# A new written-out order, with other engines and added dummy matmuls, for a fused linear-attention and MLP kernel

## The chip, the cores and the metric

The kernel runs on one core of one Trainium2 chip. A core has a matrix engine (PE, with its weight loads shown as PEld), VectorE (DVE in the profile), ScalarE (ACT), GpSimd (POOL) and SyncE (SP), which here only issues transfers. Each engine takes its instructions in the order in which the program gives them to it. The metric is the device time of one execution in microseconds (us), lower is better.

## What is computed

Inputs are r, k and v of shape (4, 8, 768, 48), that is batch, heads, sequence and head width, per-head decays w and gains u, and the weights of a small MLP on d = 384 channels. First comes a linear attention with a decaying state, then a layer norm, an MLP with ReLU and a residual sum:

```python
for t in range(S):
    kt, vt, rt = (k[:, :, t].copy(), v[:, :, t].copy(), r[:, :, t].copy())
    cur = np.einsum('bhd,bhe->bhde', u[None] * kt, vt)
    y[:, :, t] = np.einsum('bhd,bhde->bhe', rt, state + cur)
    state = w[None, :, :, None] * state + np.einsum('bhd,bhe->bhde', kt, vt)
...
mu = np.mean(x, axis=-1, keepdims=True)
var = np.mean((x - mu) ** 2, axis=-1, keepdims=True)
xn = (x - mu) / np.sqrt(var + 1e-06) * g_ln
ch = np.maximum(xn @ w_ch1, 0.0) @ w_ch2
return (x + ch).astype(np.float32)
```

## The kernel before

The sequence is cut into chunks of 128 steps. There are 6 chunks for each of 4 batches, 24 in all, numbered so that chunk i belongs to batch i mod 4 and follows chunk i - 4. Inside a chunk the recurrence is turned into matmuls: r is scaled by powers of w (Fr) and k by the inverse powers (Fk), a masked product A gives the part from within the chunk, and a state Z, carried from chunk i - 4, gives the rest. The MLP works on groups of one or two chunks (17 groups; groups 6 to 12 hold two), so that its matmuls have 128 or 256 columns.

Everything is written as small named steps, and the string `PLAN` lists them. An entry such as `SK,3,g` names the step, its index and the engine that does it: v is VectorE, s ScalarE, g GpSimd, and - means that the step has only one possible engine. A loop at the end calls one function for each entry:

```python
for step in PLAN.split():
    name, i, e = step.split(",")
    steps[name](int(i), e)
```

So the position in the string is the order on every queue at once. A load that stands late in the string is issued late by SP, and a PE step whose input is late holds up all PE steps after it. No scheduler reorders anything. The pools of buffers (`SLOTS`) say how far loads may run ahead: 11 buffers each for k, r and v.

The steps, in the order in which a chunk meets them:

- WF and WB load the row of w and spread it over 128 partitions with a matmul (line 269). LN, FR and FK make Fr and Fk from it on ScalarE. LC, CT, CP, WL, UW and UGC make the small column constants; MW, MP, MI, MM set constant tiles, among them a tile `warm` of zeros (line 222). TL loads ScalarE's function table.
- LK, LR, LV load one chunk of k, r, v (lines 326, 329, 332), in runs of 48 floats.
- SK and SR scale k and r (line 190); CV casts v to bf16 (185, 187).
- The scaled chunk is transposed. For chunks 0 to 11 TR does it on PE (line 348) and TCr, TCk or TC copy it out of PSUM. For chunks 12 to 23 TKR does it by a DMA transpose that SP issues (line 497).
- Q multiplies the two transposed parts; AT makes the product of k and r on PE (371; ATP is two of them), AM, AMa, AMb mask it (381).
- S makes the gain of the diagonal and the chunk's contribution to the state (402, 415, with 409 where an old state is added on PE). CC copies the gain, ZU and ZD update the state, VB forms the diagonal's part of the output (434).
- Y adds both parts on PE (444, 452), X brings the sum to SBUF with its row sum (459).
- XN centres it (472, 474), SQ squares it for the variance (466), RS makes the reciprocal root on GpSimd (480, 483). LT transposes on PE (512) and XT copies, or LT2 and LTD transpose by DMA (491, 487).
- UP is the first MLP matmul (527) and RL its ReLU (543, 545); the index of an UP is 16 times the group plus its part. DN is the second (557), three parts for each chunk; DA and DB do it in halves for the last chunk (574). OT adds the residual (615), STO stores (622); OA, OB, SA, SB are the halves.

The MLP's weights come in fp32, each matrix in three parts of 768 KB (LW1 at line 301, LW2 at 318). SW casts one third of a part of w1 to bf16 and multiplies it by minus the layer norm's gain. Index 3n + c means part n, rows c. It can run on any of three engines:

```python
g = g_neg[:, kc : kc + 1]
if e == "s":
    nc.scalar.activation(out=o, in_=s, func=ACT.Copy, scale=g)        # L308
elif e == "v":
    nc.vector.tensor_scalar(out=o, in0=s, scalar1=g, scalar2=None, op0=ALU.mult)        # L310
else:
    nc.gpsimd.tensor_scalar(out=o, in0=s, scalar1=g, scalar2=1.0, op0=ALU.mult, op1=ALU.mult)        # L312
```

CW casts halves of w2 parts. w2 is loaded into the buffers that w1 was loaded into, so each LW2 waits until SW has read that part. UP,2 is the first step that needs the last part of w1.

There is also a step DU, defined but not used before. It runs matmuls on the tile `warm` into a PSUM tile that nothing reads: its index divided by 4 is the number of wide ones (512 columns), the rest the number of narrow ones (128 columns).

Of the kernel before, what the change touches and what calls it, by code (L numbers as in the profile page):

```python
# [26 lines left out]
SQ,2,s SW,7,v XN,4,v XT,3,s LW2,2,- UP,2,- ZU,5,v TC,6,s LV,7,- UP,18,- SR,7,g RL,2,v CC,5,s CV,6,s LT,4,- Q,6,v UP,34,- RL,18,s LK,9,- SK,7,v S,6,-  # L27
VB,5,v TR,7,- XT,4,v CW,3,s UP,50,- TC,7,v CC,6,s RL,34,s VB,6,g RL,50,v CW,2,s UP,49,- ZU,6,v RS,2,g LV,9,- SQ,4,s Q,7,v DN,5,- RS,3,g CW,1,s Y,5,-
ATP,6,- X,5,v CW,0,g UP,48,- AM,6,v XN,5,s RS,1,g LR,9,- DN,4,- CW,5,s Y,6,- CW,4,v RL,48,s RL,49,v LT,5,- DN,6,- X,6,v LK,10,- UP,64,- CV,7,g OT,1,v
RS,0,g S,7,- LR,8,- XT,5,v DN,2,- CC,7,s ZU,7,v SQ,5,s LK,8,- DN,0,- SQ,6,s SK,9,v RS,5,g UP,81,- AM,7,v RL,64,s LK,12,- DN,1,- VB,7,g LV,8,- SR,9,v  # L30
# [632 lines left out]
```

## Time and profile before

| | us |
|---|---|
| median of 3 runs | 154.17 |
| lowest and highest | 153.74, 155.41 |
| the profiled execution | 154.56 |
| its span in the trace | 152.6 |

| engine | busy us | share of the span |
|---|---|---|
| PE | 135.7 | 89% |
| VectorE | 119.8 | 78% |
| GpSimd | 79.6 | 52% |
| ScalarE | 74.4 | 49% |

The profiled execution is 1.96 us longer than the span of its instructions; that part is start and end around them. A share of busy time is a mean over stages with different limits, so the stages are looked at one by one below. In all 28.59 MB are moved, 18.88 MB of it read from HBM.

### The profile page before, as it was taken

To read this page: it belongs to the slowest core of one execution; us is meant where nothing else is said; L and a number is where in the kernel's file an instruction comes from. 1 tells how busy PE (TensorE), PEld (TensorE's weight loads), DVE (VectorE), ACT (ScalarE), POOL (GpSimd) and SP (SyncE) were. 2 spreads that over 40 slices of the span, in tenths; PEclk is the share of its full clock that TensorE was granted. 3 is DMA by queue.
4 is the path that set the end of the run, shared out by engine and by line. 5 is a ranking of instruction groups with operands and counts; after the bars stand their busy time and mean duration, and the time that the engine had idled before them with its cause. 6 is when DMAs were issued, how large, how long until landed. Compare 5 with 4: busy or idle time off the path is not lost.

```text
span 152.6 us, 4241 instructions
## 1 busy us (share of the span) xinstructions
PE 135.7 (89%) x1680; PEld 109.3 (72%) x1680; DVE 119.8 (78%) x242; ACT 74.4 (49%) x164; POOL 79.6 (52%) x119
## 2 busy tenths in 40 slices
PE   3496479968999999998999986999999999999992
PEld 1274359858878887886797775876777878779771
DVE  3589597999989898998997859986987784687132
ACT  3553173898844925613539275541446232415610
POOL 3076777060849095994934930971901734933500
PEclk9999999999999999999999999999999999999999
...
GB/s 102 205 217 201 320 222 193 250 366 301 178 158 190 167 198 183 189 142 223 221 170 200 233 138 180 176 243 139 224 175 203 218 223 151 188 94 0 159 79 76
DMA packets 99267, 28.59 MB, mean 187 GB/s; under 512 B 94508, under 2 KB 97712, under 8 KB 99248
## 3 DMA queue, kind: packets, MB, share of 16 engines
...
HBM read 18.88 MB, written 4.72 MB: 155 GB/s over the span
## 4 chain that ended last, share of the span: by engine, by line
PE 47%; DMA 15%; POOL 14%; SPq 9%; DVE 8%; issue 5%; ACT 1%; POOLq 0%; DVEq 0%
PE hp L527 18%; PE o L557 18%; DMA kf<-in_k_dram 8%; DMA trs<-sc 6%; POOL sc L190 5%; SPq L329 4%; SPq L332 3%; POOL Z L190 3%; PE at L348 2%; DVE A L381 2%; PE at L371 2%; DVE sc L190 2%; POOL Vb L434 2%; POOL w_sb L312 1%; SPq L326 1%
## 5 line engine op out<-in xcount | busy, mean ns | idle before, releaser
L527 PE MATMUL hp<-xT,w_sb 128*128 128x128 bf16 (+1 forms) x612 | 58.7, 245 | 1.4 <-DVE w_sb L310 0.9
L527 PEld LDWEIGHTS <-w_sb 128*128 128x128 bf16 x612 | 49.7, 115 | 5.7 <-DVE w_sb L310 1.0
L557 PE MATMUL o<-w_sb,hT 128*128 128x384 bf16 x276 | 52.4, 326 | 0.0
L543 ACT ACTIVATE hT<-hp 128x512 bf16<-128x512 f32 x52 | 30.7, 595 | 32.1 <-PE hp L527 29.5
L557 PEld LDWEIGHTS <-hT 128*128 128x128 bf16 x276 | 25.1, 97 | 12.4
L434 POOL TENSOR_TENSOR Vb<-vf,cc 128x384 f32<-128x384 f32 x20 | 17.4, 869 | 24.4 <-DVE cc L187 10.5
L381 DVE TENSOR_TENSOR A<-at,mask 128x1024 bf16<-128x1024 f32 (+1 forms) x27 | 29.3, 1097 | 0.2 <-PE at L371 0.2
L615 DVE SCALAR_TENSOR_TENSOR ot<-o,rs,x 128x384 f32<-128x384 f32 x23 | 14.1, 613 | 10.5 <-PE o L557 8.0
L459 DVE SCALAR_TENSOR_TENSOR x<-s,Vb 128x384 f32<-128x384 f32 x24 | 13.2, 552 | 4.6 <-PE s L452 3.7
L190 POOL TENSOR_TENSOR sc<-rf,Fr 128x384 bf16<-128x384 f32 x12 | 12.2, 1020 | 7.6 <-DMA rf<-in_r_dram 7.5
L545 DVE TENSOR_SCALAR hT<-hp 128x512 bf16<-128x512 f32 x20 | 13.7, 685 | 1.6 <-PE hp L527 1.3
L185 ACT COPY trs<-at 128x512 bf16<-128x512 bf16 (+1 forms) x10 | 7.9, 798 | 14.3 <-PE at L348 14.3
L466 ACT ACTIVATE sqj<-x,sm 128x384 bf16<-128x384 f32 x24 | 14.7, 613 | 0.2
L348 PE MATMUL at<-ident,sc 128*128 128x128 bf16 x96 | 9.9, 263 | 4.2 <-DVE sc L190 2.2
L190 DVE TENSOR_TENSOR q<-trs 128x512 bf16<-128x512 bf16 x19 | 9.1, 483 | 4.1 <-DMA trs<-sc 3.6
L348 PEld LDWEIGHTS <-sc 128*128 128x128 bf16 x96 | 7.6, 118 | 6.6 <-DVE sc L190 3.8
L472 ACT ACTIVATE xn<-x,sm 128x384 bf16<-128x384 f32 x13 | 8.0, 615 | 8.0 <-DVE x L459 7.9
L483 POOL TENSOR_TENSOR rs<-rs,expo 128x1 f32<-128x1 f32 (+1 forms) x17 | 10.8, 638 | 1.4
L190 POOL TENSOR_TENSOR sc<-kf,Fk 128x384 bf16<-128x384 f32 x9 | 9.4, 1048 | 2.6 <-DMA kf<-in_k_dram 1.8
L190 DVE TENSOR_TENSOR sc<-kf,Fk 128x384 bf16<-128x384 f32 x15 | 10.0, 673 | 0.2 <-DMA kf<-in_k_dram 0.2
L190 DVE TENSOR_TENSOR sc<-rf,Fr 128x384 bf16<-128x384 f32 x12 | 7.6, 632 | 3.2 <-ACT Fr L280 3.2
L452 PE MATMUL s<-vv,A 128*128 128x48 bf16 x192 | 9.2, 188 | 0.8 <-DVE cc L187 0.8
...
## 6 DMA issues: line engine op xcount, KB each, us to landing
kf<-in_k_dram SPq DMA_DIRECT2D x24, 192.0 KB, 4.2
rf<-in_r_dram SPq DMA_DIRECT2D x24, 192.0 KB, 3.8
vf<-in_v_dram SPq DMA_DIRECT2D x24, 192.0 KB, 3.8
...
out_dram<-ot SPq DMA_DIRECT2D x18, 192.0 KB, 2.6
out_dram<-ot ACTq DMA_DIRECT2D x5, 192.0 KB, 2.6
trs<-sc SPq DMA_TRANSPOSE x12, 4.2
...
```

Source lines behind the costliest of these rows:

```text
L190: engines[e].tensor_tensor(out=out, in0=in0, in1=in1, op=ALU.mult)
L348: nc.tensor.transpose(out=t[:, a * HP + q, :], in_=flat[:, q, :], identity=ident[:])
L381: nc.vector.tensor_tensor(out=AA(i)[:, a:b].rearrange("p e q t -> p (e q) t"), in0=psum["at", i][:, a:b].rearrange("p e q t -> p (e q) t") ...
L434: engines[e].tensor_tensor(out=Vb(i)[:].rearrange("p (h d) -> p h d", h=H), in0=vf(i)[:], in1=cc(i)[:].unsqueeze(2).to_broadcast([P, H, D] ...
L459: nc.vector.scalar_tensor_tensor(out=xx(i)[:], in0=psum["y", i][:, :C], scalar=1.0, in1=Vb(i)[:], op0=ALU.mult, op1=ALU.add, accum_out=sm[ ...
L466: nc.scalar.activation(out=sqj[:], in_=xx(i)[:], func=ACT.Square, bias=sm[i][:], scale=-float(C), accum_out=sq[g][:, j : j + 1])
L483: nc.gpsimd.tensor_tensor(out=rs[g][:], in0=rs[g][:], in1=expo[:, :n], op=ALU.pow)
L527: nc.tensor.matmul(out=t[:, a * gw : (a + 1) * gw].rearrange("p (j t) -> p j t", j=size), lhsT=w1_sb[n][kc][:, fb::FB], rhs=xT(g)[:, :size ...
L543: nc.scalar.activation(out=o, in_=s, func=ACT.Relu)
L545: nc.vector.tensor_relu(out=o, in_=s)
L557: nc.tensor.matmul(out=psum["o", i][:, :C], lhsT=hT(g)[:, fk, j * P : (j + 1) * P], rhs=w2_sb[d][:, a, :], start=(seen == 0 and a == 0), s ...
L615: nc.vector.scalar_tensor_tensor(out=ot(i), in0=psum["o", i][:, :C], scalar=rs[g][:, j : j + 1], in1=xx(i)[:], op0=ALU.mult, op1=ALU.add,)
```

## The change

Only `PLAN` differs. All steps, indices and buffer counts stay; their order changes everywhere, many steps get another engine, and 16 DU steps are added. How many steps of a kind each engine has, where that changes:

| step | before | after |
|---|---|---|
| SW | 5 v, 3 g, 1 s | 3 v, 1 g, 5 s |
| SK | 15 v, 9 g | 10 v, 14 g |
| SR | 12 v, 12 g | 10 v, 14 g |
| Q | 19 v, 5 g | 17 v, 7 g |
| VB | 4 v, 20 g | 7 v, 17 g |
| CV | 5 v, 7 g, 12 s | 6 v, 5 g, 13 s |
| CW | 1 v, 1 g, 4 s | 2 v, 1 g, 3 s |
| XN | 4 v, 7 g, 13 s | 5 v, 6 g, 13 s |
| XT | 5 v, 3 s | 3 v, 5 s |
| TCk | 2 v, 2 s | 3 v, 1 s |
| CC | 11 v, 13 s | 12 v, 12 s |
| RL | 20 v, 52 s | 19 v, 53 s |
| CP | v | s |
| SB | issued by s | issued by SP |

The DU steps, in order: two of index 8 ahead of WB; 8, 10, 8, 26 between WB and CT, TR,0; 8 and 4 ahead of TR,1; 2 ahead of S,0; then 8 ahead of S,1, S,2, Y,1, LT,0, Y,2, TR,5 and, last, behind UP,2.

The place of some transfers in SP's order, counting from 1:

| transfer | before | after |
|---|---|---|
| LK,0 and LR,0 | 1, 2 | 4, 3 |
| LK,2 and LR,1 | 7, 4 | 1, 2 |
| LK,3 | 14 | 8 |
| LW1,0, LW1,1, LW1,2 | 15, 16, 25 | 13, 18, 22 |
| LT2,6 | 41 | 47 |
| LK,16 | 67 | 61 |
| TKR,12, TKR,13 | 52, 55 | 53, 57 |
| TKR,14, TKR,15 | 61, 64 | 68, 70 |
| TKR,16, TKR,18 | 73, 83 | 77, 87 |

The diff, with the ramp, the stretch around TKR,12 to TKR,16 and the end:

```diff
-WF,0,s LK,0,- MW,0,v MM,0,g MP,0,v LC,0,s LR,0,- MI,0,g LK,1,- TL,0,s WB,0,- LR,1,- LN,0,s LV,0,- FR,0,s FK,0,s LR,2,- SR,0,v LC,1,s SK,0,v TR,0,-
-LK,2,- SK,1,v LC,2,s LV,2,- SR,1,v TCr,0,s TCk,0,v TR,1,- LV,1,- Q,0,v CT,0,- TCr,1,v LR,4,- SR,2,g TCk,1,v AT,0,- CP,0,v WL,0,s LV,3,- SK,2,v UW,0,g
-TR,2,- AMa,0,v CV,0,s LR,5,- Q,1,g AMb,0,v S,0,- TCk,2,s LR,3,- AT,1,- TCr,2,s ZU,0,v CV,1,g CV,2,s CC,0,v Q,2,v LK,3,- VB,0,g S,1,- AMa,1,v AT,2,-
-LW1,0,- CC,1,s ZU,1,v CV,3,s SR,4,g LW1,1,- VB,1,v S,2,- LK,5,- ZU,2,v SR,3,g CC,2,v AMb,1,v LK,4,- Y,0,- SK,3,g X,0,v TR,3,- AMb,2,v VB,2,g AMa,2,v
-Y,1,- LR,6,- XN,0,g TCk,3,s X,1,v UGC,0,s TCr,3,s LT,0,- SW,0,g SW,2,v Y,2,- XT,0,s Q,3,v SW,1,g AT,3,- XN,1,s X,2,v SR,5,v LT,1,- XN,2,s LV,4,-
-UP,0,- AM,3,v SQ,1,s XT,1,v S,3,- SW,3,v RL,0,s LK,6,- LT,2,- SK,5,g SW,4,s CC,3,v SW,5,v UP,16,- XT,2,v LK,7,- ZU,3,v SK,4,g TR,5,- LV,5,- VB,3,g
-TR,4,- TC,5,v LV,6,- Y,3,- TC,4,s UP,17,- X,3,v LW1,2,- CV,4,v RL,16,s Q,5,v ATP,4,- LR,7,- SK,6,v XN,3,s UP,33,- Q,4,v RL,17,s AM,4,v LW2,1,- S,4,-
-RL,33,s UP,32,- LW2,0,- CV,5,s ZU,4,v RL,32,s SR,6,v CC,4,s AM,5,v SQ,3,s Y,4,- VB,4,g UP,1,- SQ,0,s X,4,v TR,6,- RL,1,s SW,6,g SW,8,v LT,3,- S,5,-
...
-CV,9,v DN,8,- Q,9,v TC,8,s XN,7,v UP,66,- LT2,6,- OT,2,v RL,82,s S,9,- RL,66,s ATP,8,- ZU,9,v CV,8,s LR,11,- DN,18,- CC,9,v Q,8,v SQ,7,s VB,9,g
-LR,12,- AM,8,v S,8,- DN,17,- STO,1,- ZD,9,g LV,10,- DN,16,- ZU,8,v CC,8,v LK,13,- AM,9,v SR,10,g UP,80,- LR,15,- Y,8,- VB,8,g OT,4,v UP,101,- SK,11,v
-TR,10,- LV,11,- X,8,v DN,21,- TC,10,s SR,11,v XN,8,g Y,9,- LV,12,- DN,22,- RL,80,s Q,10,v CV,10,g X,9,v TR,11,- SK,12,g DN,20,- TC,11,v XN,9,s LR,13,-
-S,10,- OT,5,v UP,96,- ZD,8,g CC,10,s RL,101,s Q,11,v LT2,8,- ATP,10,- RL,96,s SR,12,g ZU,10,v UP,98,- AM,10,v DN,13,- VB,10,g RL,98,s TKR,12,- UP,97,-
-AM,11,v CV,11,g Y,10,- CV,12,g RL,97,s LR,14,- UP,100,- SR,13,g X,10,v LK,14,- DN,12,- SK,13,v RS,6,g DN,14,- RL,100,v TKR,13,- S,11,- OT,3,v UP,116,-
-ZD,10,g ZU,11,v UP,113,- LK,15,- RL,116,s CC,11,v Q,12,v VB,11,g STO,3,- Y,11,- RL,113,v UP,115,- LV,13,- XN,10,v DN,30,- LV,14,- SR,14,v RL,115,s
-X,11,v UP,99,- XN,11,g S,12,- RL,99,s DN,28,- ZU,12,v Q,13,g LT2,10,- ATP,12,- SK,14,v CC,12,s DN,29,- VB,12,g AM,12,v TKR,14,- UP,114,- CV,13,s
-SR,15,g UP,112,- SQ,8,s OT,7,v STO,2,- Y,12,- CV,14,s SK,15,v ZD,12,g DN,26,- STO,4,- RL,112,s RL,114,v DN,25,- TKR,15,- X,12,v ZD,11,g UP,133,-
-AM,13,v S,13,- LV,15,- XN,12,g DN,24,- CC,13,s RL,133,v LR,17,- UP,129,- LK,16,- ZU,13,v UP,117,- OT,6,v RL,129,s ZD,13,v Y,13,- RL,117,s LR,16,-
-UP,131,- VB,13,v SQ,10,s Q,14,v DN,32,- Q,15,v RL,131,s LK,17,- X,13,v UP,130,- SQ,9,s S,14,- SQ,12,s RS,7,g ATP,14,- CC,14,v XN,13,s UP,128,- VB,14,g
-AM,14,v STO,5,s LT2,12,- RL,130,s DN,33,- SK,16,g RL,128,s DN,34,- ZU,14,v CV,15,s LV,16,- SR,16,g UP,132,- OT,8,v LR,18,- Y,14,- SR,17,v SK,17,g
...
-DN,89,- UP,258,- OT,22,v DB,1,- RL,258,v STO,22,- DA,1,- DB,0,- DB,2,- DA,2,- OB,23,v DA,0,- SB,23,s OA,23,v SA,23,s
+WF,0,s LK,2,- MW,0,v MI,0,g MP,0,v TL,0,s DU,8,- LR,1,- MM,0,g LR,0,- DU,8,- LC,1,s LK,0,- WB,0,- LC,0,s LR,2,- DU,8,- LC,2,s LN,0,s DU,10,- LK,1,-
+FR,0,s FK,0,s DU,8,- SR,1,g LV,0,- DU,26,- SR,0,g LK,3,- SK,0,v LV,1,- SK,2,v CT,0,- SR,2,v TR,0,- LV,2,- CP,0,s SK,1,v UGC,0,s DU,8,- UW,0,g TCr,0,s
+TCk,0,v DU,4,- LR,5,- TR,1,- CV,0,s Q,0,v TR,2,- LR,3,- TCk,1,v DU,2,- S,0,- TCr,2,s TCr,1,v CC,0,v LW1,0,- WL,0,s AT,0,- Q,1,g TCk,2,v AT,1,- LK,4,-
+CV,1,s ZU,0,v DU,8,- SK,3,g AMb,0,v LK,5,- S,1,- DU,8,- AMa,0,v CC,1,s Q,2,g LV,3,- AMa,1,v CV,2,g ZU,1,v VB,0,g AMb,1,v S,2,- AT,2,- CC,2,v ZU,2,v
+SR,3,g SR,5,v LR,4,- Y,0,- VB,2,g TR,3,- X,0,v DU,8,- TCr,3,s AMb,2,v LW1,1,- XN,0,g TCk,3,s Y,1,- VB,1,v LR,6,- SW,1,s DU,8,- AMa,2,v SW,0,s LV,4,-
+SW,2,v LT,0,- X,1,v DU,8,- Q,3,v XN,1,s LK,6,- XT,0,v Y,2,- SK,5,v CV,3,s AT,3,- SR,4,g X,2,v DU,8,- TR,5,- AM,3,v XN,2,s UP,0,- SK,4,g LW1,2,- TC,5,v
+LT,1,- S,3,- LV,5,- XT,1,s LT,2,- CC,3,v ZU,3,v RL,0,s VB,3,g TR,4,- XT,2,s LR,7,- Y,3,- TC,4,v UP,16,- SW,5,s SW,4,g CV,4,s Q,4,v SR,6,g ATP,4,-
+LK,7,- X,3,v RL,16,s UP,32,- SW,3,s AM,4,v XN,3,g S,4,- RL,32,s Q,5,g UP,17,- ZU,4,v LW2,1,- LT,3,- AM,5,v UP,33,- RL,17,s SK,6,g LV,6,- CC,4,s XT,3,s
+UP,1,- RL,33,s VB,4,v Y,4,- LW2,0,- RL,1,s SW,6,v UP,49,- X,4,v CV,5,s TR,6,- SW,7,s SW,8,v S,5,- TC,6,v XN,4,s LW2,2,- UP,2,- SQ,1,s SK,7,v LV,7,-
+DU,8,- SR,7,v RL,49,s RS,1,g ZU,5,v RL,2,s TR,7,- Q,6,v SQ,2,s LT,4,- LK,9,- UP,34,- XT,4,v CC,5,s UP,48,- RL,34,v CV,6,s S,6,- TC,7,s VB,5,v UP,18,-
...
+LK,12,- TR,8,- CV,8,s X,7,v DN,8,- TC,8,s CV,9,v STO,0,- Q,9,v DN,9,- LR,12,- Q,8,v S,9,- DN,10,- LV,11,- RL,66,v CC,9,s SQ,4,s ZU,9,v ATP,8,- LK,13,-
+SQ,5,s RS,4,g OT,2,v S,8,- UP,82,- AM,8,v CC,8,s SK,10,g RL,80,s LR,13,- DN,18,- SQ,3,s XN,7,v VB,8,g DN,16,- RL,82,s ZU,8,v LT2,6,- DN,17,- SR,11,v
+SK,11,g Y,8,- OT,4,v LV,10,- UP,81,- X,8,v LR,14,- SR,12,g UP,50,- AM,9,v XN,8,s STO,1,- TR,11,- VB,9,g RL,50,s LK,14,- DN,20,- RL,81,v TC,11,s
+SR,10,g Y,9,- LV,12,- SK,12,v DN,21,- ZD,8,g TR,10,- X,9,v TKR,12,- UP,97,- TC,10,s XN,9,v ZD,9,g UP,99,- RL,97,v CV,10,s LR,15,- ATP,10,- Q,10,v
+CV,11,s SR,13,g LV,13,- RL,99,s UP,101,- AM,10,v SQ,7,s LT2,8,- S,10,- UP,96,- RS,5,g RL,101,s ZU,10,v DN,22,- RL,96,s CC,10,v SK,13,v VB,10,g Y,10,-
+OT,5,v UP,100,- TKR,13,- Q,11,v RS,3,g DN,13,- X,10,v RL,100,s AM,11,v DN,14,- Q,12,g STO,5,- S,11,- STO,2,- UP,98,- ZU,11,v LK,15,- DN,12,- CV,12,v
+RL,98,s CC,11,v LK,16,- VB,11,g Y,11,- CV,13,s OT,3,v UP,112,- SR,14,g X,11,v STO,3,- UP,116,- RL,112,v STO,4,- XN,10,g DN,30,- ZD,10,v RL,116,s
+LV,14,- SR,15,g ATP,12,- XN,11,s S,12,- LT2,10,- DN,28,- CC,12,s ZU,12,v RS,6,g UP,115,- AM,12,v LR,16,- VB,12,g DN,29,- RL,115,s LR,17,- Q,13,g
+UP,117,- SQ,8,s OT,7,v Y,12,- SK,14,v RL,117,s DN,24,- SK,15,g SQ,9,s X,12,v TKR,14,- UP,114,- AM,13,v ZD,12,g DN,26,- LR,19,- DN,25,- RL,114,v
+ZD,11,g TKR,15,- S,13,- UP,113,- CC,13,s RS,7,g ZU,13,v UP,129,- LV,15,- RL,113,s OT,6,v VB,13,g Y,13,- LK,17,- SQ,12,s CV,14,v DN,34,- XN,12,s
...
+RS,15,g LT,23,- STO,20,s DN,86,- XT,23,s DN,84,- UP,258,- OT,21,v UP,256,- RL,258,s DN,90,- RL,256,s DN,89,- STO,21,s UP,257,- DN,88,- RL,257,s DB,0,-
+OT,22,v DB,2,- DB,1,- STO,22,s DA,0,- OB,23,v DA,1,- DA,2,- SB,23,- OA,23,v SA,23,s
```

More of the change, by code (lines that the diff above doesn't have):

```diff
@@ L27 @@
[L27 to L30, printed above, removed]
@@ new lines @@
+CV,16,g LV,19,- DN,38,- RL,149,v VB,15,g LR,18,- Y,15,- OT,9,v UP,144,- Q,16,v LK,19,- DN,41,- X,15,v RL,144,s ZD,15,v UP,145,- XN,15,g S,16,-
+RL,145,s ATP,16,- LT2,14,- ZU,16,v CC,16,s DN,40,- Q,17,v SK,18,v VB,16,g DN,42,- LV,18,- AM,16,v STO,9,- UP,147,- SR,19,g LK,20,- UP,148,- OT,10,v
+RL,147,s CV,19,v CV,17,g Y,16,- STO,7,s DN,45,- RL,148,s X,16,v SR,18,g UP,160,- AM,17,v SK,19,g TKR,18,- S,17,- DN,46,- RL,160,v UP,161,- XN,16,v
+TKR,19,- CC,17,v ZU,17,v UP,162,- VB,17,g RL,161,s Y,17,- SQ,14,s LK,21,- DN,44,- X,17,v RL,162,s LR,20,- UP,163,- OT,11,v XN,17,g UP,165,- Q,18,v
```

35 lines of the change are left out of this document (17 added, 18 removed).

## The prediction

> **What bounds the kernel now.** I read the page's slices first, then busy time by stretch, then the chain of waits, then single engines and queues where the chain points.
>
> ```profile
> PE   3496479968999999998999986999999999999992
> PEclk9999999999999999999999999999999999999999
> ```
> ```profile
> 10.00:15.00 5.00, 3.42 (x46) 2.45 (x44) 4.67 (x11) 2.83 (x7) 3.70 (x5) 1.00 1.06 208
> 20.00:25.00 5.00, 4.27 (x50) 3.67 (x48) 4.88 (x11) 3.37 (x7) 4.52 (x5) 1.00 0.91 182
> 40.00:50.00 10.00, 10.00 (x157) 8.28 (x157) 9.28 (x18) 5.25 (x12) 7.27 (x13) 1.00 0.81 161
> 50.00:60.00 10.00, 10.00 (x143) 8.00 (x141) 9.17 (x23) 5.51 (x11) 4.79 (x6) 1.00 0.80 178
> 90.00:100.00 10.00, 8.21 (x98) 6.81 (x97) 7.93 (x16) 6.07 (x15) 4.30 (x7) 1.00 0.89 166
> 110.00:120.00 10.00, 10.00 (x107) 7.75 (x105) 8.58 (x19) 4.91 (x13) 3.04 (x6) 1.00 1.04 192
> ```
>
> The columns of the second view are the stretch, its length, then busy time (instructions) of PE, PEld, DVE, ACT and POOL, granted clock, DMA share, GB/s. The kernel has a ramp and a full stage. In the ramp VectorE is the tight engine (4.88 of 5 us at 20 to 25) and PE is part idle. From 40 us PE is busy 10.00 of 10, except where a wait shows, as in 90 to 100, where it loses 1.79; the DMA engines stand at 0.80 in 50 to 60 and at 1.04 in 110 to 120, so DMA is the second limit. The end therefore moves with two things: the moment from which PE is full, and the holes afterwards.
>
> ```profile
> 12.39 4.34 DMA kf<-in_k_dram
> 17.94 0.62 PE at L348 x4
> 19.81 2.26 POOL w_sb L312 x2
> 22.12 1.36 PE hp L527 x11
> 24.23 1.28 PE hp L527 x12
> 25.51 1.60 PE at L348 x16
> 33.08 1.60 DVE w_sb L310 x2
> 34.72 1.48 PE hp L527 x23
> 39.36 0.65 PE o L557 x4
> 46.07 0.67 PE hp L527 x12
> 86.08 5.74 DMA trs<-sc
> ```
>
> In this view (start, length, what) the same PE work has two prices: 12 matmuls of UP take 1.28 us at 24.23 and 0.67 at 46.07, 107 ns against 56. The granted clock does not show this: it is 1.00 in the stretches 10 to 15 and 110 to 120 alike. So a half rate in the ramp has to be read from matmul times, not from that column. The ramp's chain goes over a k transfer (12.39), transposes at half rate, two w1 scalings on GpSimd (19.81), UP and transposes at half rate, then two w1 scalings on VectorE (33.08) ahead of UP,2 (34.72). Later a TKR (86.08, 5.74 us) is in the chain.
>
> **The change part by part.** All steps of the reference remain; only the 16 DU steps are new.
>
> *Warm-up matmuls.* They are 33 wide ones (512 columns) and 6 narrow (128). Warm, a wide one costs 0.217 us (an estimate: 4 of 384 columns take 0.65 at 39.36, scaled to 512); cold 0.427 (4 times 107 ns). Most lie where PE waits anyway. One DU,8 stands behind UP,2, close to the full stage, where I hide nothing: 2 times 0.217 = 0.43 lost. What they may bring is the half rate's end: the PE pieces in the chain of the ramp are 0.62 + 1.36 + 1.28 + 1.60 = 4.86 us, and half of it is 2.43. Bounds: 0 to 2.43 gained; I take all of it, since the kernel itself runs at 56 ns once PE is dense.
>
> *What they delay.*
>
> ```profile
> 0.93 0.11 DVE L222 MEMSET warm<- 128x64 uint32 x1
> 2.35 1.61 PE L269 MATMUL s<-w_row,one 1*128 1x384 f32 x2 [2.35 <-DMA w_row<-in_w_dram]
> 5.86 1.11 PE L348 MATMUL at<-ident,sc 128*128 128x128 bf16 x8 [1.89 <-DVE sc L190]
> ```
>
> WB started at 2.35 when the row of w had landed, ended at 3.96, and Fr and Fk hang on it. Now four wide dummies stand ahead of it. They can start when the tile they read is set, at 1.04, and end at 1.04 + 4 x 0.427 = 2.75, so WB and all factors come 0.4 late. TR,0, at 5.86 before, now stands behind WB (2.75 + 1.61 = 4.36), 12 wide and 4 narrow dummies (5.55 cold, 2.83 warm) and CT: it starts between 7.2 and 9.9, and with the change of rate midway at about 8.5, which is 2.6 late. Behind it in PE's queue are TR,1, TR,2 and all of S, AT and Y. Not all of it is carried on: chunks 0 to 2 then follow closely, where before PE waited between them. VectorE is what hands it on, and its list up to AM,3 is nearly the same work, only begun later; I carry 1.0 us, with 0 and 2.6 as ends.
>
> *w1's scaling.*
>
> ```profile
> L310 DVE TENSOR_SCALAR w_sb<-w_f,g_neg 128x512 bf16<-128x512 f32 x5 | 4.1, 841 | 0.3 <-DMA w_f<-in_moe_w_ch_dram 0.3
> L308 ACT ACTIVATE w_sb<-w_f,g_neg 128x512 bf16<-128x512 f32 x1 | 0.7, 712 | 0.0
> ```
>
> GpSimd loses two of three SW steps, VectorE two of five, ScalarE gets four. On the chain GpSimd's pair, 2.26, becomes two of ScalarE, 2 x 0.712 = 1.42: 0.84 gained. VectorE's two moved steps, 2 x 0.841 = 1.7, free the tight engine of the ramp; I count none of it as a gain (bounds 0 and 1.7), because it is the slack out of which VectorE works off the rest of the 2.6 above.
>
> *Loads of the ramp.*
>
> ```profile
> 13.14 1.46 SPq L301 DMA_DIRECT2D w_f<-in_moe_w_ch_dram  x2
> 25.98 1.31 SPq L301 DMA_DIRECT2D w_f<-in_moe_w_ch_dram  x1
> ```
> ```profile
> kf<-in_k_dram SPq DMA_DIRECT2D x24, 192.0 KB, 4.2
> ```
>
> LW1,0 and LW1,1 were SP's 15th and 16th transfers (13.14), LW1,2 the 25th (25.98). They are now the 13th, 18th and 22nd; LK,3, which ended the wait at 12.39, moves from 14th to 8th. A load is 192 KB, or 0.196 MB; at the 208 GB/s of the stretch 10 to 15 it takes 0.945 us of the DMA engines. Three loads fewer ahead of LW1,2 are 2.8 us, so UP,2 could come at 32 instead of 34.72 if the engines follow. They do by this sum: 2.43 + 0.84 - 1.0 = 2.3. The two routes agree within their error, and I take 2.5 for the ramp, bounds 0 and 4. Less the DU,8 it is 2.1 at 40 us, where PE has no slack to lose it.
>
> *The full stage.* PE's order moves little against the chunks, so what counts is whether SP's queue delivers in time. TKR,14 becomes SP's 68th transfer instead of the 61st, TKR,15 the 70th instead of the 64th, TKR,16 77th for 73rd, TKR,18 87th for 83rd; on the other side LK,16 comes 61st for 67th. Three of the seven more ahead of TKR,14 are loads (2.8 us), four are stores (3.8 if each costs as much as a load).
>
> ```profile
> 73.67 1.23 SPq L497 DMA_TRANSPOSE trs<-sc  x1
> ```
> ```profile
> 81.53 0.24 PE L402 MATMUL s<-uwI,q 128*128 128x2 bf16 x4
> 92.87 0.24 PE L402 MATMUL s<-uwI,q 128*128 128x2 bf16 x4 [1.78 <-DVE x L459]
> 105.82 0.25 PE L402 MATMUL s<-uwI,q 128*128 128x2 bf16 x4 [0.33 <-DVE q L190]
> ```
>
> TKR,14 was issued at 73.67. If it takes as long as the slow one at 86.08, it lands at 79.4, and S,14 came at 81.53: 2.1 us of cover or more. That cover is just what the ramp's 2.1 us use up, so any lateness in the queue shows. Against that stand the idle DMA time in 50 to 60 (0.2 x 10 = 2 us), which earlier loads can fill, and the waits at 92.87 and 105.82 (1.78 and 0.33), which hung on TKR,16 and TKR,18 or what precedes them, and to which LK,16 now leaves 6 transfers more of room. Bounds: -2.1 (both holes gone) to +2.1 (the whole ramp gain given back); I take 0, since lateness at TKR,14 and room at LK,16 are of one size.
>
> *Moves between engines in the full stage.* VectorE gives five SK, two SR and two Q to GpSimd and gets three VB; an engine that is not last costs nothing, and the place where GpSimd could be is a rival below. The last store half goes from ScalarE's queue to SP's, which has nothing else then: 0.
>
> Sum: the profiled execution took 154.56 (span 152.6, 1.96 around it). 154.56 - 2.5 + 0.43 + 0 = 152.5; the median, 154.17, lies 0.39 below the profiled one, hence 152.1.
>
> One rule speaks against this sum. The Trainium skill, "TensorE: Matmul & The Clock Gate", Part 1, says that the clock doubles after about 3.4 us of sustained activity in a free-running window and calls the ramp's penalty under 1% of a typical span; by that the warm-up would bring at most 1.5 us and the sum would be 153.0. Rows 24.23 and 46.07 agree with its two rates; that a ramp stays at the low one until some 26 us is more than it allows for.
>
> **The rivals.**
>
> *DMA takes it all* (0.22). The ramp gains, and S,14 to S,18 wait for TKR. For it: the DMA share of 1.04 in 110 to 120. Against: 2 us idle in 50 to 60. Price: 2.1 given back, 154.2.
>
> *GpSimd becomes the bound in the middle* (0.14), the one on the slow side.
>
> ```profile
> 57.00:83.00 26.00, 17.96 (x24) 1.00 1.05 189
> ```
> ```profile
> L434 POOL TENSOR_TENSOR Vb<-vf,cc 128x384 f32<-128x384 f32 x4 | 3.6, 907 | 0.0
> L190 POOL TENSOR_TENSOR sc<-rf,Fr 128x384 bf16<-128x384 f32 x3 | 3.2, 1060 | 0.0
> L474 POOL TENSOR_SCALAR xn<-x,sm 128x384 bf16<-128x384 f32 x3 | 2.0, 658 | 3.3 <-DVE x L459 3.3
> L187 POOL CAST vv<-vf 128x384 bf16<-128x384 f32 x3 | 1.4, 501 | 0.6 <-DMA vf<-in_v_dram 0.6
> L483 POOL TENSOR_TENSOR rs<-rs,expo 128x2 f32<-128x2 f32 x2 | 1.4, 696 | 0.2
> L190 POOL TENSOR_TENSOR q<-trs 128x512 bf16<-128x512 bf16 x1 | 1.2, 1152 | 0.0
> L190 POOL TENSOR_TENSOR sc<-kf,Fk 128x384 bf16<-128x384 f32 x1 | 1.0, 1002 | 0.0
> L480 POOL TENSOR_SCALAR rs<-sq 128x2 f32<-128x2 f32 x2 | 0.6, 288 | 4.0 <-ACT sqj L466 4.0
> ```
>
> Between VB,8 and RS,7 its list gets one SK, two SR, one VB, one Q and two RS more and three CV and two XN fewer: 1.0 + 2.1 + 0.9 + 1.15 + 2.0 - 1.5 - 1.3 = 4.3 us on top of 17.96 in 26. The 8.0 us of idle cover that only if they lie in the right places; 3.3 and 4.0 of them were waits for VectorE and ScalarE in an in-order queue. If half of those waits go, the idle time holds the 4.3 and nothing is lost. If they all stay, 0.7 us is free and 3.6 fall on SR, SK, TKR and S, up to 1.78 more where a late TKR leaves PE a hole like that at 92.87: 152.1 + 3.6 = 155.7 to 157.5, 156.6 in the middle. It decides from about 25 busy of 26 us there.
>
> *The dummies delay and do not warm* (0.12). TR,0 is 2.6 late, matmuls between 10 and 22 us stay at 107 ns, the 2.43 is missing, the scaling's 0.84 stays: 154.17 + 2.6 - 0.84 = 155.9. For it: 46 matmuls in 10 to 15 kept PE busy 3.42 of 5 us and were slow all the same. Against: the first dummies are gapless for over 3 us. The same page, Part 4, says that transposes do not count as activity, which would make the gaps between dummies longer than they look; nothing in this trace tells that apart.
>
> *More than forecast* (0.10): the ramp's 2.1 holds and the holes 1.78 and 0.33 vanish as well: 154.17 - 4.2 = 150.0.
>
> **How the numbers follow.** The forecast, with 0.42, is 152.1, its own range 150.7 to 152.6. For this kernel 1% (1.5 us) is about what a measurement can tell from none. Faster by more than that: 0.42 + 0.10 = 0.52. Within: 0.22. Slower: 0.14 + 0.12 = 0.26. The range runs from 149.8 to 156.8, from the best case to just over GpSimd's middle price, and leaves out about 0.15: half of each of these two and a little for what I did not see.
>
> **What would show it.** In the changed profile: matmuls of TR,1 and later before 20 us at 56 ns per 128 columns; UP,2 near 32; LK,3 out of the chain; PE full from about 38; S,14 waiting for trs at most 1 us; GpSimd under 25 of 26 us in the stretch VB,8 to RS,7. Wrong if the early matmuls stay at 107 ns, if UP,2 is not earlier, or if PE's holes after 40 us sum to more than the 2.1 of the two shown here (1.78 and 0.33).

## The result, and the profile after

Over 20 executions of each, beside one another, the changed kernel has a median of 153.19 us (151.54 to 156.43) against 154.23 (152.94 to 157.92), 1.0 us less. The ratio is 0.9914, 95% interval 0.9884 to 0.9943, which is 1.3 us. A second set gave 152.47 against 153.92, ratio 0.991 (0.988 to 0.9941). Medians are over all executions, while the ratios leave out each kernel's longer ones (17 of the 29 of before in the set of the first four experiments), so that there a ratio can stand as much as 0.7% above that of the medians. Where the two say different things, both are given; kernels measured on different chips are compared by either of them, not by their times.

The profiled execution took 151.54 us, the shortest of its 20, and that of before 154.56, just above its median. The spans, 149.8 and 152.6, therefore differ by more than twice what the kernels differ by, and a part of what follows is the spread of single executions.

The slices of the page of the changed kernel, and below them busy time by stretch, with the columns as before:

```profile
PE   7997696999999999999999999899999999999992
PEclk9999879999999999999999999999999999999999
DMA  5999999999899999999999999999996967411112
```
```profile
10.00:15.00 5.00, 3.99 (x56) 2.42 (x54) 4.08 (x10) 2.84 (x8) 2.94 (x3) 1.00 0.96 213
15.00:20.00 5.00, 3.61 (x44) 2.52 (x45) 5.00 (x11) 1.40 (x3) 4.16 (x6) 0.75 0.98 233
20.00:25.00 5.00, 3.94 (x45) 2.52 (x44) 5.00 (x10) 2.54 (x5) 2.13 (x2) 0.90 1.08 260
40.00:50.00 10.00, 9.93 (x126) 7.46 (x124) 8.28 (x20) 6.43 (x15) 4.64 (x8) 1.00 0.95 183
50.00:60.00 10.00, 9.80 (x137) 7.67 (x136) 9.96 (x17) 6.15 (x14) 9.33 (x11) 1.00 0.98 207
90.00:100.00 10.00, 9.35 (x115) 7.61 (x113) 7.38 (x16) 3.62 (x9) 6.24 (x7) 1.00 1.07 203
120.00:130.00 10.00, 10.00 (x126) 7.92 (x124) 8.01 (x17) 3.31 (x9) 2.30 (x4) 1.00 0.67 169
```

PE is busy from 1 us on, which is dummies. The granted clock, 1.00 everywhere before, shows 0.75 and 0.90 at 15 to 25: the rate went up early and fell back for a while. VectorE is full, 5.00 of 5, just there. The DMA engines stand at 0.98 in 50 to 60, where they stood at 0.80, and have 0.67 left to do at 120 to 130, where they were full.

PE's instructions in order of time, at the places the prediction named, and all its waits after 45 us (start, length, what; in brackets the wait ahead and who ended it):

```profile
9.10 0.62 PE L349 MATMUL at<-ident,sc 128*128 128x128 bf16 x8
17.53 1.04 PE L349 MATMUL at<-ident,sc 128*128 128x128 bf16 x8 [0.15 <-POOL sc L191]
33.31 0.83 PE L528 MATMUL hp<-xT,w_sb 128*128 128x128 bf16 x12
```
```profile
57.44 0.82 PE L558 MATMUL o<-w_sb,hT 128*128 128x384 bf16 x4 [0.19 <-DVE hT L546]
67.55 1.50 PE L528 MATMUL hp<-xT,w_sb 128*128 128x256 bf16 x12 [0.34 <-DMA xT<-xn]
95.89 0.85 PE L528 MATMUL hp<-xT,w_sb 128*128 128x256 bf16 x6 [0.65 <-DMA xT<-xn]
```

TR,0 starts at 9.10 and its 8 matmuls take 0.62 us instead of 1.11. At 17.53 the same work takes 1.04: this is the stretch of the lower clock. UP,2 runs from 33.31; before, its first matmul ran at 33.63 and the others from 34.72, after 0.88 us of waiting for w1. The holes at S,16 and S,18 (1.78, 0.33) are gone, and with them one of 0.45 at S,12; 0.19, 0.34 and 0.65 have come, the last two for LT2 transposes. No S waits for a TKR.

To compare kernels in whose orders PE does different work, I count PE's lost time: the start of a step less the full-rate price of all PE work ahead of it. The prices come from the chain (12 matmuls of UP 0.67, four of DN 0.65 and so on); the price of the dummies is not taken off, so they count as lost. Within one order the difference between two kernels is simply that between their starts of the step. In the table, "to S,7" is the ramp and "S,7 to S,23" the full stage, each from one profiled execution.

| kernel | lost to S,7 | lost S,7 to S,23 | profiled, us | median, us | ratio to before |
|---|---|---|---|---|---|
| before | 21.2 | 4.6 | 154.56 | 154.23 | |
| changed | 20.0 | 3.1 | 151.54 | 153.19 | 0.9914 |
| changed, again | 20.3 | 2.9 | 151.63 | 152.47 | 0.991 |

The ramp gained 0.9 to 1.2 us, the full stage 1.5 to 1.7. Together that is some 2.7, about twice what the medians show (1.0 and 1.5): both profiles of the changed kernel are of short executions, so how the gain of the medians is split is less sure than the table looks.

### The profile page after: what moved, and what is told of

Same layout as the page of the kernel before. It is cut to its first block, busy times and chain, and to the rows that moved or that the text cites. A ratio compares the mean times of both kernels' runs of the same rounds, so it can differ in the third digit from the quotient of the medians.

```text
span 149.8 us, 4315 instructions
## 1 busy us (share of the span) xinstructions
PE 140.6 (94%) x1719; PEld 108.8 (73%) x1719; DVE 117.2 (78%) x235; ACT 77.4 (52%) x170; POOL 83.9 (56%) x120
## 3 DMA queue, kind: packets, MB, share of 16 engines
q10 hardware_dynamic: 896, 1.09, 2.0%
## 4 chain that ended last, share of the span: by engine, by line
PE 62%; DVE 18%; DMA 8%; issue 3%; ACT 3%; POOL 3%; DVEq 0%; POOLq 0%
PE o L558 23%; PE hp L528 21%; DMA xT<-xn 6%; DVE A L382 5%; PE o L259 4%; DVE x L460 3%; PE at L372 3%; DMA trs<-sc 2%; PE at L349 2%; DVE sc L191 2%; DVE trs L188 2%; PE s L453 2%; POOL sc L191 2%; PE s L445 1%; ACT sqj L467 1%
## 5 line engine op out<-in xcount | busy, mean ns | idle before, releaser
L528 PE MATMUL hp<-xT,w_sb 128*128 128x128 bf16 (+1 forms) x612 | 56.7, 242 | 1.0 <-DMA xT<-xn 1.0
L435 POOL TENSOR_TENSOR Vb<-vf,cc 128x384 f32<-128x384 f32 x17 | 15.0, 882 | 12.7 <-DVE cc L188 7.1
L191 POOL TENSOR_TENSOR sc<-rf,Fr 128x384 bf16<-128x384 f32 x14 | 15.4, 1104 | 5.4 <-ACT Fr L281 3.7
L191 POOL TENSOR_TENSOR sc<-kf,Fk 128x384 bf16<-128x384 f32 x14 | 15.1, 1085 | 1.6 <-PE s L416 1.6
L481 POOL TENSOR_SCALAR rs<-sq 128x1 f32<-128x1 f32 (+1 forms) x17 | 3.7, 215 | 17.5 <-ACT sqj L467 16.6
L259 PE MATMUL o<-warm 128*128 128x512 bf16 x33 | 12.1, 490 | 1.1 <-DVE warm L223 1.1
L191 DVE TENSOR_TENSOR sc<-kf,Fk 128x384 bf16<-128x384 f32 x10 | 8.3, 842 | 4.8 <-DMA kf<-in_k_dram 4.8
L191 POOL TENSOR_TENSOR q<-trs 128x512 bf16<-128x512 bf16 x7 | 8.5, 1218 | 5.8 <-DVE cc L188 2.1
L186 ACT COPY trs<-at 128x1024 bf16<-128x1024 bf16 (+1 forms) x9 | 7.3, 823 | 6.5 <-PE at L349 6.3
L475 POOL TENSOR_SCALAR xn<-x,sm 128x384 bf16<-128x384 f32 x6 | 3.7, 624 | 9.6 <-DVE x L460 9.4
```

Source lines behind the costliest of these rows:

```text
L191: engines[e].tensor_tensor(out=out, in0=in0, in1=in1, op=ALU.mult)
L259: nc.tensor.matmul(out=warm_ps[0][:], lhsT=warm[:], rhs=warm[:].unsqueeze(1).to_broadcast([P, 4, P]), start=True, stop=True)
L435: engines[e].tensor_tensor(out=Vb(i)[:].rearrange("p (h d) -> p h d", h=H), in0=vf(i)[:], in1=cc(i)[:].unsqueeze(2).to_broadcast([P, H, D] ...
L528: nc.tensor.matmul(out=t[:, a * gw : (a + 1) * gw].rearrange("p (j t) -> p j t", j=size), lhsT=w1_sb[n][kc][:, fb::FB], rhs=xT(g)[:, :size ...
```

## The experiments

All runs stand against the kernel before on the same chip, 6 to 20 executions each.

**The dummies.** Two kernels take them out of the new order: the first all 16, the second only the ten behind TR,0.

```diff
-DU,8,-
...
-DU,26,-
...
-DU,8,-
```

> The new order with all 16 DU steps taken out. Theory A (the warm-up pays): UP and the transposes of the ramp run at 107 ns per 128 columns again until about 26 us; 2.43 us of PE time return on the chain, less about 1.0 us for TR,0, which is held by its inputs and no longer by dummies: about 1.4 us slower than the changed kernel, 154.6 us, ratio to before 1.003. Rival B (VectorE paces the ramp, PE's rate is worth little there): within 0.4 us of the changed kernel, ratio 0.989 to 0.994, UP,2 still near 33.3 us.

```diff
 DU,26,-
...
 TR,0,-
...
-DU,8,-
...
-DU,4,-
...
-DU,8,-
```

> The new order with only the six DU steps ahead of TR,0; the ten later ones are out. Theory A: the rate is at its full value from about 8.5 us, falls back once the dummies stop and stays low from about 15 to 26 us; slower than the changed kernel by about 1.0 us, ratio to before 0.998. Rival B: the later dummies keep nothing that matters and only occupy PE; within 0.4 us of the changed kernel or up to 0.4 us faster (the DU behind UP,2 gone), ratio 0.987 to 0.994.

A third puts the 16 into the old order, at the same neighbours.

```diff
+DU,8,- DU,8,-
 WB,0,-
...
+DU,8,- DU,10,- DU,8,- DU,26,-
 TR,0,-
...
 UP,2,-
+DU,8,-
```

> The old order and engines with the same 16 DU steps put at the same neighbours (ahead of WB; ahead of TR,0, TR,1, S,0, S,1, S,2, Y,1, LT,0, Y,2, TR,5; behind UP,2). Theory A: the old ramp's chain loses 2.43 us of slow PE time and gains 1.0 us from the later TR,0 and 0.43 us of the last DU: 1.0 us faster than before, ratio 0.9935. Rival B: TR,0 comes 2.6 us later, VectorE paces the rest: 1 to 2.6 us slower than before, ratio 1.006 to 1.017.

| kernel | lost to S,7 | lost S,7 to S,23 | profiled, us | median, us | ratio to before |
|---|---|---|---|---|---|
| new order, no dummies | 19.8 | 6.2 | 154.44 | 153.76 | 0.9986 (0.9942 to 1.003) |
| new order, front dummies only | 21.3 | 3.0 | 152.72 | 153.19 | 1.0011 (0.9976 to 1.0045) |
| old order, with dummies | 21.5 | 4.6 | 155.32 | 157.94 | 1.025 (1.0177 to 1.0323) |

The ramp answers plainly. Without any dummy it is not later but as early as in the changed kernel (S,7 at 42.57 for 42.78), although its matmuls run at 107 ns until about 25 us. From S,0 to S,3, some 10 to 25 us, the changed kernel takes 13.96 us, the one without dummies 13.63 and the one with the front ones alone 13.62, whatever the rate. VectorE is full there, also where the clock (third column from the end) is at one half, as with the front ones alone:

```profile
15.00:20.00 5.00, 2.91 (x43) 2.47 (x44) 4.92 (x12) 0.17 (x1) 5.00 (x6) 0.72 1.04 224
20.00:25.00 5.00, 2.85 (x38) 2.29 (x37) 5.00 (x12) 3.45 (x7) 2.79 (x4) 0.50 0.93 251
```

So the half rate itself costs next to nothing in the ramp: VectorE sets the pace. The dummies put S,0 1.2 us later (11.40 for 10.23), and the kernel without them is still 1.5 us ahead at S,3 (23.86 for 25.36). By S,7 it has lost this lead to its loads. Its chain of waits then stands on a load of k (first fence), the changed kernel's on VectorE (second):

```profile
26.04 7.31 DMA kf<-in_k_dram
33.37 1.04 DVE sc L185 x2
```
```profile
28.39 1.04 DVE A L382
33.14 0.63 DVE trs L188
```

With the front dummies alone S,7 is 1.5 us later than with none and 1.2 later than with all. That is not the price of the ten later ones, since the difference to the changed kernel stands already at S,0 (12.80 for 11.40). The eight wide dummies ahead of TR,0, the same in both kernels, took 3.62 us there and 2.35 in the changed kernel (second row), because the rate rose later in that execution:

```profile
6.38 3.62 PE L253 MATMUL o<-warm 128*128 128x512 bf16 x8
6.39 2.35 PE L259 MATMUL o<-warm 128*128 128x512 bf16 x8
```

In the second profile of the changed kernel they took 3.07. From S,0 to S,7 the kernel with the front ones takes 31.22 us, the changed one 31.38 and 30.91. In the time, the ratio has 1.5 us for the ten later dummies (1.0011 for 0.9914) and the medians have nothing (0.9938 for 0.9933), so no worth of theirs is shown.

In the old order the ramp does not move either (21.5 for 21.2). Why that kernel's median is 3.8 us higher its profile, taken in the shortest of its 6 executions, does not show.

The whole time says something else than the ramp, so no-dummies went in again beside the unchanged new order, with a third kernel in which only the long front dummy is shortened.

> The changed kernel once more, as the mark for the three others of this call and for the spread of its profile: ratio to before 0.988 to 0.997, 152.7 to 153.7 us; time that PE has lost up to S,7 near 20.0 us and from there to S,23 between 3 and 5 us if the first profile was a lucky one, 3.1 again if not.

> The new order without its 16 DU steps once more, beside the new order on the same chip. Theory V (VectorE paces the ramp; the front dummies cost what the later ones save): within 0.4 us of the changed kernel in this call, UP,2 at 32.5 to 33.5 us. Rival A (the warm-up pays): 0.6 us or more slower than the changed kernel in this call.

```diff
-DU,26,-
+DU,8,-
```

> The new order with the one long DU ahead of TR,0 cut from index 26 to 8 (four wide and two narrow dummies fewer, about 1.0 us at the full rate). Theory V: TR,0 at 8.0 instead of 9.1 us, VectorE's copies behind it 0.8 us earlier, UP,2 near 32.5 us, and 0.3 to 0.8 us faster than the changed kernel in this call. Rival D (what the ramp gains, the transfers of the full stage take back): UP,2 as early, but within 0.3 us of the changed kernel.

| kernel | lost to S,7 | lost S,7 to S,23 | profiled, us | median, us | ratio to before |
|---|---|---|---|---|---|
| new order again | 20.3 | 2.9 | 151.63 | 152.47 | 0.991 (0.988 to 0.9941) |
| no dummies again | 19.8 | 5.8 | 154.12 | 153.96 | 1.0029 (0.9997 to 1.0061) |
| shorter front dummy | 22.8 | 3.5 | 154.76 | 153.22 | 0.9952 (0.9916 to 0.9989) |

Without dummies the kernel is 1.5 us slower than with them on the same chip, the size that theory A gave, but not at A's place: the ramp is as early, and in the profiled executions 2.9 us more are lost behind it. PE's steps of this kernel (no dummies, again), and SP's issue of LT2,8 there and in the changed kernel:

```profile
31.91 0.80 PE L522 MATMUL hp<-xT,w_sb 128*128 128x128 bf16 x11 [0.24 <-ACT w_sb L303]
58.85 1.50 PE L522 MATMUL hp<-xT,w_sb 128*128 128x256 bf16 x12 [0.57 <-DMA xT<-xn]
69.37 1.50 PE L522 MATMUL hp<-xT,w_sb 128*128 128x256 bf16 x12 [1.83 <-DMA xT<-xn]
```
```profile
63.66 3.70 SPq L486 DMA_TRANSPOSE xT<-xn  x1
```
```profile
63.69 1.72 SPq L492 DMA_TRANSPOSE xT<-xn  x1
```

UP,2 is some 1.4 us earlier than in the changed kernel (its second matmul at 31.91, there the first at 33.31), and then PE waits 0.57 and 1.83 us for the transposes LT2,6 and LT2,8. In the first run without dummies it waits 1.27 us for LT2,8. SP needs 3.70 us to issue LT2,8 instead of 1.72. It is the same step at the same time; the DMA engines were fuller in the stretch ahead of it, 50 to 60 (1.17, lower row), than with dummies (0.98):

```profile
15.00:20.00 5.00, 3.20 (x40) 2.43 (x38) 4.92 (x11) 2.30 (x4) 2.25 (x3) 1.00 0.96 226
50.00:60.00 10.00, 9.41 (x133) 7.43 (x132) 9.33 (x17) 6.04 (x14) 9.02 (x11) 1.00 1.17 199
```

The upper row is for the clock, which reads 1.00 though the matmuls are slow. With the front dummies alone the DMA engines stand at 0.96 in that stretch and PE does not wait at LT2,8, so the six ahead of TR,0 are enough for this. Why the transfers bunch there without them I cannot say.

The shorter front dummy brings TR,0 to 8.21 and the early UPs forward, and then PE waits for loads, 1.50 us for a chunk of v and in UP,2 for w1:

```profile
8.21 0.62 PE L344 MATMUL at<-ident,sc 128*128 128x128 bf16 x8
33.26 0.33 PE L411 MATMUL s<-vv,sc 128*128 128x96 bf16 x4 [1.50 <-ACT vv L181]
33.89 0.82 PE L523 MATMUL hp<-xT,w_sb 128*128 128x128 bf16 x11 [0.24 <-ACT w_sb L304]
```
```profile
30.32 0.49 DVE L306 TENSOR_SCALAR w_sb<-w_f,g_neg 128x512 bf16<-128x512 f32 x1 [0.67 <-DMA w_f<-in_moe_w_ch_dram]
```

ScalarE's cast of v waited 2.37 us for its load, SW,6 0.67 for the third part of w1, and most of UP,2 comes at 33.89, not at 32.5: an earlier ramp runs into its loads here too. This profile is of the longest of its 12 executions, so only the order of events is read from it. The median is 0.75 us above the unchanged order's: theory V's gain did not come, rival D's "no gain" did, and a little more.

**The scaling of w1.** Once put back in the new order (the diff shown), once moved alone in the old (the same diff read upwards):

```diff
-SW,0,s SW,1,s SW,2,v SW,3,s SW,4,g SW,5,s SW,6,v SW,7,s SW,8,v
+SW,0,g SW,1,g SW,2,v SW,3,v SW,4,s SW,5,v SW,6,g SW,7,v SW,8,v
```

> The new order with the nine SW steps on their old engines (five VectorE, three GpSimd, one ScalarE). Theory A (the moved scaling is part of the gain): 0.84 us on the chain at SW,0 and SW,1, and up to 1.7 us of VectorE: 0.8 to 2.0 us slower than the changed kernel, ratio to before 0.997 to 1.004. Rival C (the earlier transfers of w1 make the gain, any engine would do): within 0.4 us of the changed kernel, ratio 0.989 to 0.994.

> The old order with the nine SW steps on their new engines (five ScalarE, three VectorE, one GpSimd). Theory S (taking the scaling off GpSimd and VectorE is worth the same 1.6 us that putting it back into the new order cost): 0.8 to 1.6 us faster than before, ratio 0.990 to 0.995, UP,2 at 33 to 34 us. Rival P (it pays only where the order around it was written for it, since ScalarE's list in the old order holds other work there): within 0.4 us of before or slower, ratio 0.997 to 1.005.

| kernel | lost to S,7 | lost S,7 to S,23 | profiled, us | median, us | ratio to before |
|---|---|---|---|---|---|
| new order, old scaling | 23.3 | 3.0 | 154.82 | 154.81 | 1.0061 (1.0026 to 1.0095) |
| old order, new scaling | 20.5 | 4.8 | 153.97 | 154.0 | 0.9991 (0.9951 to 1.0032) |

In the new order the old scaling costs 3.3 us of the ramp in the profiled executions. Of these 1.2 stand at S,0 (12.56 for 11.40), ahead of any scaling, where the rate rose later; at S,3 only 0.4 of them are left (25.75 for 25.36), so some 2.9 hang on the scaling. The time is 1.5% longer by the ratios (1.0061 for 0.9914, some 2.3 us) and 1.1% by the medians (1.7 us); the kernel is slower than before: theory A, at its upper end or above. In the old order the new scaling gains 0.7 us of ramp and nothing that the time shows: rival P.

**The ramp's loads alone.** The first 25 transfers of the old order in about the new sequence:

```diff
-LK,0 LR,0 LK,1 LR,1 LV,0 LR,2 LK,2 LV,2 LV,1 LR,4 LV,3 LR,5 LR,3 LK,3 LW1,0 LW1,1 LK,5 LK,4 LR,6 LV,4 LK,6 LK,7 LV,5 LV,6 LW1,2
+LK,2 LR,1 LR,0 LK,0 LR,2 LK,1 LV,0 LK,3 LV,1 LV,2 LR,5 LR,3 LW1,0 LV,3 LR,4 LW1,1 LK,5 LK,4 LR,6 LV,4 LK,6 LW1,2 LV,5 LV,6 LK,7
```

> The old order and engines; only the first 25 transfers of SP come in about the new sequence (LK,3 8th, LW1,0 13th, LW1,1 16th, LW1,2 22nd). Theory C (the earlier transfers are the ramp's gain): UP,2 from 34.7 to about 33 us, 0.8 to 1.5 us faster than before, ratio 0.990 to 0.995. Rival V (VectorE and GpSimd, not the transfers, pace the ramp): UP,2 within 0.5 us of 34.7, time within 0.4 us of before, ratio 0.997 to 1.003.

156.83 us, ratio 1.0161 (1.0094 to 1.0229). PE's lost time to S,7 is 24.0, and UP,2 comes 2.8 us later than before, not earlier:

```profile
37.47 1.48 PE L522 MATMUL hp<-xT,w_sb 128*128 128x128 bf16 x23 [0.91 <-DVE w_sb L305]
```

Neither theory had this: the old order scales chunk 0 first, whose k and r now arrive third and fourth, and everything behind waits.

**SP's order in the full stage alone.** Five loads go ahead of LT2,6 in the old order:

```diff
-LT2,6,- LR,11,- LR,12,- STO,1,- LV,10,- LK,13,- LR,15,-
+LR,11,- LR,12,- LV,10,- LK,13,- LR,15,- LT2,6,- STO,1,-
```

> The old order with one thing of the new: five loads (LR,11, LR,12, LV,10, LK,13, LR,15) go ahead of LT2,6, at which SP waited until 52 us while the DMA engines stood at 0.80. Theory M (the gain behind the ramp is SP's order, which fills this idle time): DMA share 0.95 or more at 40 to 60, PE's holes after 40 us fall from 2.6 to about 1 us, 0.7 to 1.5 us faster than before, ratio 0.990 to 0.995. Rival E (the new engines of the full stage make it): within 0.4 us of before, ratio 0.997 to 1.003.

155.46 us, ratio 1.0108 (1.0052 to 1.0163). The DMA engines are indeed fuller in 50 to 60, but LT2,6 now stands behind those loads, and PE waits for it where it did not wait before:

```profile
50.00:60.00 10.00, 7.51 (x106) 5.98 (x104) 8.05 (x19) 3.72 (x8) 5.57 (x7) 0.99 1.22 187
```
```profile
59.08 0.82 PE L522 MATMUL hp<-xT,w_sb 128*128 128x256 bf16 x6 [2.49 <-DMA xT<-xn]
```

Filling the idle DMA time in this way gains nothing; whether another way would is not shown. (This profile is of an execution 3.8 us above the median, so the length of the hole may belong to it alone.)

**The engines of the full stage.** The new order with the old engines for chunks 8 to 23, for 82 steps and for the 19 of SK, SR and Q among them:

```diff
-SK,9,g SK,12,v SK,15,g ... SR,8,v SR,14,g ... Q,12,g Q,22,v ... RL,97,v XN,8,s CC,10,v VB,13,g ...
+SK,9,v SK,12,g SK,15,v ... SR,8,g SR,14,v ... Q,12,v Q,22,g ... RL,97,s XN,8,g CC,10,s VB,13,v ...
```

> The new order with the old engines for the steps of chunks 8 to 23 (82 steps: SK, SR, CV, TC, Q, CC, ZD, VB, XN, XT and RL of groups 6 and later). Theory M (SP's order makes the gain behind the ramp): within 0.4 us of the changed kernel, ratio to before 0.989 to 0.996. Rival E (the moves to GpSimd make it): 0.8 us or more slower than the changed kernel, ratio 0.997 or more.

> The new order with the old engines for SK, SR and Q of chunks 8 to 23 alone (19 steps), where the run with all 82 steps put back lost 3.8 us. Theory K (the scalings of k and r taken by GpSimd free VectorE where its list is full): at least half of it, 1.9 us or more slower than the changed kernel in this call. Rival L (it is the many small swaps of RL, XN, CC and CV, which fit the order): 1.0 us slower or less.

| kernel | lost to S,7 | lost S,7 to S,23 | profiled, us | median, us | ratio to before |
|---|---|---|---|---|---|
| all 82 put back | 20.2 | 7.8 | 156.84 | 156.96 | 1.0252 (1.0204 to 1.0299) |
| SK, SR, Q put back | 20.5 | 4.5 | 153.57 | 154.09 | 1.0016 (0.998 to 1.0052) |

The ramp stays, and the full stage loses 4.7 us more with all 82, 1.4 to 1.6 with the 19. By the ratios all 82 cost 3.4% (1.0252 for 0.9914), 5.2 us, as the two profiled executions have it too (156.84 for 151.54); by the medians (1.0207 for 0.9933) it is 2.7%, 4.2 us. Between the two theories the second run lies in the middle: 1.6 us above the unchanged order measured beside it (152.47), where K wanted 1.9 or more and L at most 1.0. Who holds PE up is seen in its waits between 50 and 90 with all 82 put back, and DMA in the stretch 80 to 90 is not full:

```profile
54.64 0.34 PE L440 MATMUL s<-Z,trs 128*128 128x96 bf16 x4 [0.50 <-DVE ZS L424]
58.05 0.37 PE L448 MATMUL s<-vv,A 128*128 128x48 bf16 x8 [0.25 <-DVE A L377]
58.65 0.82 PE L553 MATMUL o<-w_sb,hT 128*128 128x384 bf16 x4 [0.22 <-DVE hT L541]
62.13 0.81 PE L523 MATMUL hp<-xT,w_sb 128*128 128x256 bf16 x6 [0.30 <-ACT hT L539]
66.05 1.46 PE L553 MATMUL o<-w_sb,hT 128*128 128x384 bf16 x8 [0.23 <-DVE ot L611]
69.56 0.34 PE L440 MATMUL s<-Z,trs 128*128 128x96 bf16 x4 [0.48 <-DVE cc L183]
80.37 0.82 PE L523 MATMUL hp<-xT,w_sb 128*128 128x256 bf16 x6 [0.65 <-DVE hT L541]
81.96 0.81 PE L553 MATMUL o<-w_sb,hT 128*128 128x384 bf16 x4 [0.41 <-DVE ot L611]
86.43 0.81 PE L523 MATMUL hp<-xT,w_sb 128*128 128x256 bf16 x6 [0.23 <-DVE hT L541]
```
```profile
80.00:90.00 10.00, 8.99 (x104) 7.30 (x103) 7.73 (x18) 5.62 (x14) 5.14 (x8) 1.00 0.78 167
```

Eight of the nine are ended by VectorE, for RL, A, ZU, OT and CC, one by ScalarE. Over the stretch 50 to 90 VectorE is busier in the changed kernel (the lower row) than with all 82 put back (the upper), yet only one of the changed kernel's three waits, 0.19 us, is VectorE's:

```profile
50.00:90.00 40.00, 36.61 (x440) 28.35 (x437) 33.55 (x63) 18.46 (x45) 28.26 (x38) 1.00 0.89 187
```
```profile
50.00:90.00 40.00, 39.47 (x487) 31.95 (x485) 37.01 (x69) 23.12 (x53) 31.45 (x40) 1.00 1.07 206
```

So it is which step stands where in VectorE's list, not how full the engine is. All 82 put back lose more than the kernel before does in its own order (7.8 for 4.6): the old engines do not fit the new order. The new engines in the old order were not tried.

None of the variants was faster than the changed kernel.

## Why the prediction came out as it did

The forecast was 152.1 us; the medians are 153.19 and 152.47. Faster by more than 1%, which had a chance of 0.52, is missed by 0.1% of the time by the ratios; what came had 0.22. By lost time the ramp was forecast 1.0 us too large and the full stage 1.6 us too small; the sum came out near because these go in opposite directions, and that part is luck.

*The warm-up, 2.43.* Wrong in the ramp. The step "the PE pieces in the chain of the ramp ... half of it is 2.43" took every PE piece in the chain for time that would be saved. Without dummies the ramp is as early (19.8 for 20.0 and 20.3): at half rate VectorE set the pace up to S,3, and loads behind it. A chain goes through the engine that ended last at each step; with VectorE full, the next thing ended barely later. What the Trainium skill, "TensorE: Matmul & The Clock Gate", Part 1, says of the ramp's penalty, under 1% of a typical span, stood nearer to it than my sum. Behind the ramp the dummies are worth something, by a way that the sum did not have.

*The dummies' delay.* TR,0 came at 9.10, and at 9.81 in the second profile; forecast was 8.5. The 1.0 us carried to the end of the ramp measured 0.2 to 0.5 against no dummies (S,7 at 42.78 and 43.03 for 42.57 and 42.58), and 1.5 with the front ones alone, where the rate rose last. The rival "the dummies delay and do not warm" had the matmuls between 10 and 22 us stay at 107 ns. It was half right: the rate rose, fell at 17.5 for some 3.5 us and rose again.

*The scaling, 0.84, with VectorE's 1.7 not counted.* Too small: some 2.9 us of ramp hang on it in the new order. A part is that the price of a step on VectorE was read as a mean, 841 ns, where 470 and 1,010 stand side by side (last section).

*The ramp as a whole, 2.1.* Measured 0.9 to 1.2. UP,2 came 1.4 us earlier, not 2.7. "Three loads fewer" did bring the third part of w1 forward (issued at 23.41, 25.98 before), but VectorE came to its scaling only at 31.80, without a wait for the load.

*The full stage, 0, between -2.1 and +2.1.* Measured -1.5 to -1.7, inside the bounds. TKR,14 as SP's 68th transfer delayed nothing, since S,14 had no wait; the hole at S,16 went, as the bound of -2.1 allowed. Whether the reason given, room for LK,16 in SP's queue, was the cause no run shows: the one that moved loads ahead moved five others, and made the old order slower.

*"An engine that is not last costs nothing: 0."* This step does not hold. With the old letters in the new order PE waits for VectorE eight times between 50 and 90, and it costs 4.2 to 5.2 us; the profiled execution loses 4.7 between S,7 and S,23. SK, SR and Q make about a third of it; which of the other 63 steps make the rest was not tried. That the change of engines brought the full stage's 1.5 to 1.7 is possible by this, but it is not shown: the 4.2 to 5.2 are the price of a misfit, and taking out the dummies undoes the gain of that stage as well.

*The rivals.* GpSimd did not become the bound, though its load was forecast well. From VB,8 to RS,7, now 52.3 to 77.7, it was busy 22.69 of 25.4 us, where the forecast of 17.96 + 4.3 makes 22.3:

```profile
52.30:77.70 25.40, 22.69 (x29) 1.00 1.10 205
```

In the second profile it was busy 23.36, and one wait of PE, 0.45 us at 58.44, was ended by it. DMA did not take the ramp's gain by late TKRs; loads did hold the ramp where it came earlier still, without dummies and with the shorter front one.

*The signs listed.* TR,1 and later before 20 us at 56 ns: in part. From their start to the next, the 16 matmuls of TR,1 and TR,2 take 1.09 us (68 ns each), the 8 of TR,3, at 17.53, 0.82 (103 ns). UP,2 near 32: 33.31. LK,3 out of the chain: yes. S,14 waiting at most 1 us: it does not wait. PE full from 38: 9.93 of 10 us in 40 to 50. The holes after 40 us sum to 1.18, less than the 2.1 of the two before (2.56 with the one at S,12).

What stays open: why the front dummies are worth 0.6 to 1.8 us (by medians and ratios) behind the ramp, by way of which transfers, why the same dummies make the old order 3.8 us slower, and which part of the new order brings the gain of the full stage.
